# fp32 weight and Q/K loads by hardware DMA with casts on GpSimd, a mask added by a matmul, and global rows kept per parity, in a fused attention and feed-forward kernel

## The chip, the cores and the metric

The kernel runs on one core of a Trainium2 chip. The metric is device microseconds (us) of one execution. Before the change it takes 426.68 us in the median of 3 runs (426.24 to 429.5). Engines are named as the profile names them: PE (TensorE matmul), PEld (TensorE weight load), DVE (VectorE), ACT (ScalarE), POOL (GpSimd), SP (the queue that issues most DMAs).

## The reference, cut to what matters

```python
# attention: 8 batches, 8 heads, 576 positions, head dim 64
mask = np.abs(pos[:, None] - pos[None, :]) <= 32           # a band ...
mask = mask | is_global[:, None] | is_global[None, :]      # ... and 8 global positions
attn = softmax(where(mask, scale * q @ k.T, -1e9)); o = attn @ v
x = o.transpose(0, 2, 1, 3).reshape(4608, 512)
# feed-forward on 4608 tokens, 512 -> 1536 -> 512
ffn_out = (gelu(x @ w_gate) * (x @ w_val)) @ w_out
out = x + sigmoid(x @ w_res) * ffn_out
```

All inputs are fp32 in memory; the kernel computes in bf16.

## The kernel before: the parts that matter

The 4608 tokens are nine chunks of 512. For each chunk TensorE does twelve steps of the inner projections (`ffn_in`, matmuls into `g_ps` and `v_ps`), then sixteen pieces of the outer part (`r_ps`, three thirds of `f_ps` for each of four token tiles), and between those pieces the attention of the next chunk. Attention of a chunk needs scores `sc`, the scores of the global rows `sg` (keys of the global positions, `kgz`) and `ss` (queries of the global positions, `qgz`), and the values `nd`. A `gather` is an indirect DMA, issued by GpSimd, that fetches the rows at the global positions (`kgf`, `qgf`, `vgf`); `vgb` and `vgs` are the global rows of v in bf16 and spread over the heads. `hot` marks the global positions and `far` holds squared distances to them; both serve the masks.

```python
# loads that cast, issued by GpSimd
def load_gate_cols(n0, n1):
    for src, dst in ((moe_w_gate, wg_t), (moe_w_val, wv_t)):
        nc.gpsimd.dma_start(dst[:, :, n0:n1], src.rearrange(...)[:, :, n0:n1])
...
kgz = const.tile([128, B, NP, 128], BF16, ...)      # global rows of all 8 batches
qgz = const.tile([128, B, NP, 16], BF16, ...)
...
def shift_v(b):                                     # vo: ve moved by 64 partitions, by DMA
    nc.sync.dma_start(vo[b % 2][0:64, 0:4], ve[b % 2][64:128, 0:4])
    nc.sync.dma_start(vo[b % 2][64:128, 0:4], ve[b % 2][0:64, 1:5])
...
# scores: exp, then VectorE multiplies by the 0/1 mask
nc.scalar.activation(mine, sc, ACTF.Exp, bias=0.0, scale=SCALE)
nc.vector.tensor_tensor(mine, mine, view(maskw, ...), ALU.mult)
...
# spread_qk, once for batches 2 to 7 in chunk 1, by VectorE (k) and ScalarE (q)
(nc.scalar.copy if what == "q" else nc.vector.tensor_copy)(view(big, ...), view(tg, ...))
```

The softmax here doesn't subtract the row's maximum and nothing guards it: scores larger than these inputs give would overflow.

Of the kernel before, what the change touches and what calls it, by code (L numbers as in the profile page):

```python
# [23 lines left out]
def kernel(  # L24
# [46 lines left out]
    ve = pair_of([128, 5, H, VG], "ve")  # L71
    vo = pair_of([128, 4, H, VG], "vo")
# [5 lines left out]
    vgs = const.tile([128, B, H * VG], BF16, name="vgs", tag="vgs")  # L78
# [14 lines left out]
    def load_v(b):  # L93
        t = ve[b % 2]
        for c in range(5):
            p0, p1 = (32, 128) if c == 0 else (0, 96) if c == 4 else (0, 128)
            s0 = 128 * c - 32
            nc.gpsimd.dma_start(t[p0:p1, c, :, 0:D],  # L98
                                v[b].rearrange("h s d -> s h d")[s0 + p0:s0 + p1])

    def shift_v(b):
        nc.sync.dma_start(vo[b % 2][0:64, 0:4, :, :], ve[b % 2][64:128, 0:4, :, :])
        nc.sync.dma_start(vo[b % 2][64:128, 0:4, :, :], ve[b % 2][0:64, 1:5, :, :])

    def load_gate_cols(n0, n1):
        for src, dst in ((moe_w_gate, wg_t), (moe_w_val, wv_t)):
            nc.gpsimd.dma_start(dst[:, :, n0:n1], src.rearrange("(kt p) n -> p kt n", p=128)[:, :, n0:n1])


    RPP = 6  # L110
    QP = S // RPP
    STG = 2 * RPP * D
    raw = {"q": ht.rearrange("p a b -> p (a b)").bitcast(F32), "k": wo_t.rearrange("p a b -> p (a b)").bitcast(F32)}
# [3 lines left out]
    for p in range(NP):  # L117
        for src, what in ((q, "q"), (k, "k")):
            nc.sync.dma_start(raw[what][0:QP, STG * p:STG * p + STG].rearrange("c (h n) -> c h n", h=2),
                              src[0, 2 * p:2 * p + 2].rearrange("h (c r) d -> c h (r d)", r=RPP))  # L120

# [29 lines left out]
    kgz = const.tile([128, B, NP, 128], BF16, name="kgz", tag="kgz")  # L151
    qgz = const.tile([128, B, NP, 16], BF16, name="qgz", tag="qgz")

    def zero_qk(i):
        for u in range(2):
            zero_wide(qz[i], 64 - 64 * u, 64, u * S, [[2 * S, NP], [1, S]])
        zero_wide(kt[i], 0, 128, 0, [[S + 64, NP], [1, 32]])
        zero_wide(kt[i], 0, 128, 32 + S, [[S + 64, NP], [1, 32]])

    def zero_rest(i, eng):  # L160
        eng.memset(ve[i][:, :, :, D:VG], 1.0)
        eng.memset(ve[i][0:32, 0, :, :], 0.0)
        eng.memset(ve[i][96:128, 4, :, :], 0.0)
        eng.memset(gt[i][:, 0:64], 0.0)
        eng.memset(gt[i][:, 64 + S:128 + S], 0.0)
        eng.memset(ptg[i][:, :, 64 * (i % 2):64 * (i % 2) + 64], 0.0)

    def zero_globals(b0, b1):
        zero_wide(kgz, 0, 128, b0 * NP * 128, [[1, (b1 - b0) * NP * 128]])
        zero_wide(qgz, 0, 128, b0 * NP * 16, [[1, (b1 - b0) * NP * 16]])  # L170
# [5 lines left out]
    nc.scalar.copy(view(pt.bitcast(F32), 0, 128, 32, [[64, H * CH], [1, 32]]),  # L176
                   view(none, 0, 128, 0, [[0, H * CH], [0, 32]]))
# [3 lines left out]
    zero_qk(0)  # L181
    zero_globals(0, 2)
# [14 lines left out]
    zero_rest(0, nc.gpsimd)  # L197
    load_v(0)
    gather("v", 0)
    load_gate_cols(0, 512)  # L200


    gpc = const.tile([128, 1], F32, name="gpc", tag="gpc")
    nc.vector.tensor_copy(gpc, gpi)
    ngp = const.tile([128, 1], F32, name="ngp", tag="ngp")
    nc.vector.tensor_single_scalar(ngp, gpc, -1.0, ALU.mult)
    hot = const.tile([128, S], BF16, name="hot", tag="hot")
    nc.vector.tensor_scalar(hot, iota_f, gpc, None, ALU.is_equal)
    for n in range(1, B // 2):
        nc.vector.tensor_single_scalar(idx[:, n:n + 1], idx[:, 0:1], float(2 * H * S * n), ALU.add)  # L210
    far = const.tile([128, S], F32, name="far", tag="far")
# [5 lines left out]

    def masks():
        nc.vector.tensor_tensor(diag, blk[:, 0:8], blk[:, 8:16], ALU.add)
# [4 lines left out]
        for w0, w1 in ((0, NW), (NW, NWM)):  # L224
            n = w1 - w0
            nc.vector.tensor_tensor(maskw[:, w0:w1, :], nong[:, 0:64 * n].rearrange("p (w c) -> p w c", c=64),
                                    view(band, 0, 128, 0, [[0, n], [1, 64]]), ALU.mult)

    def hot_rows(i):
        r0 = 64 - 64 * (i % 2)  # L230
        nc.scalar.copy(gt[i][r0:r0 + 64, 64:64 + S], hot[r0:r0 + 64, :])
# [11 lines left out]
    def spread_qk(n0, n1):  # L243
        nn = n1 - n0
        for what, big, pstep in (("k", kgz, 144), ("q", qgz, 16)):
            tg = pss.tile([128, nn, 128], BF16, name="tg", tag="sc")
            for n in range(nn):
                nc.tensor.transpose(tg[:, n, :], twice[what][:, n0 + n, :, :].rearrange("p a d -> p (a d)"), ident)
            width = big.shape[2] * big.shape[3]
            for e in range(2):  # L250
                shift = 64 * e if what == "k" else 0
                for u in range(2):
                    (nc.scalar.copy if what == "q" else nc.vector.tensor_copy)(
                        view(big, 64 * u, 64, (2 * n0 + e) * width + shift + 8 * u,
                             [[2 * width, nn], [pstep, NP], [1, NG]]),
                        view(tg, 64 * u, 64, 64 * e + 8 * u, [[128, nn], [16, NP], [1, NG]]))
# [4 lines left out]
    def spread_vg(b, eng):  # L261
        r0 = 64 * (b % 2)
        eng.tensor_tensor(vgs[r0:r0 + 64, b, :].rearrange("p (h e) -> p h e", e=VG),
# [12 lines left out]
    def cast_pair(p, what):  # L276

        if p < 3:
            dst = (q_st if what == "q" else k_st).rearrange("c r n -> c (r n)")[0:QP, STG * p:STG * p + STG]
        else:  # L280
            o = 0 if what == "q" else STG
            dst = xtok[1].rearrange("c t n -> c (t n)")[0:QP, o:o + STG]
        src = raw[what][0:QP, STG * p:STG * p + STG].rearrange("c (u r d) -> c r u d", u=2, r=RPP)
        (nc.scalar.copy if what == "q" else nc.vector.tensor_copy)(dst.rearrange("c (r u d) -> c r u d", r=RPP, u=2), src)
        return dst

    def turn_pair(p, what, src):
        ps = bank([128, RPP, QP], f"t{what}0", BF16)
        for r in range(RPP):
            nc.tensor.transpose(ps[:, r, :], src[:, 128 * r:128 * r + 128], ident[0:QP, 0:QP])  # L290
        if what == "q":
            nc.scalar.copy(qt[0][:, p, :].rearrange("c (s r) -> c s r", r=RPP), ps.rearrange("c r s -> c s r"))
        else:
            nc.vector.tensor_copy(kt[0][:, p, 32:32 + S].rearrange("c (s r) -> c s r", r=RPP),
                                  ps.rearrange("c r s -> c s r"))
# [13 lines left out]
    def global_scores(b):  # L309
        sg = psn.tile([128, 2, 512], F32, name="sg", tag="nd")  # L310
        for hf in range(2):
            for p in range(NP):
                nc.tensor.matmul(sg[:, hf, 0:288], kgz[:, b, p, :], qt[b % 2][:, p, 288 * hf:288 * hf + 288],  # L313
                                 start=(p == 0), stop=(p == NP - 1))
        ss = pss.tile([128, 5, 64], F32, name="ss", tag="sc")
        for c in range(5):
            for p in range(NP):
                nc.tensor.matmul(ss[:, c, 16 * p:16 * p + 16], kt[b % 2][:, p, 128 * c:128 * c + 128],  # L318
                                 qgz[:, b, p, :], start=True, stop=True)
# [11 lines left out]
    def global_rows(b):  # L331
# [6 lines left out]
        nc.vector.tensor_tensor(vgs[rq:rq + 64, b, :].rearrange("p (a h e) -> p a h e", a=2, e=VG),  # L338
# [4 lines left out]
    def scores(c, quad, p):  # L343
        sc = bank([128, 4, 2, 64], "sc") if c == 0 else pss.tile([128, 4, 2, 64], F32, name="sc", tag="sc")
        for n in range(4):
            b, i = divmod(CH * c + 4 * quad + n, NW)
            nc.tensor.matmul(sc[:, n, :, :], kt[b % 2][:, p, 64 * i:64 * i + 128],  # L347
                             qz[b % 2][:, p, :, 64 * i:64 * i + 64], start=True, stop=True)
        mine = view(pt, 0, 128, (2 * p * CH + 4 * quad) * 128, [[128, 4], [CH * 128, 2], [1, 64]])
        nc.scalar.activation(mine, sc, ACTF.Exp, bias=0.0, scale=SCALE)  # L350
        i0 = (CH * c + 4 * quad) % NW
        nc.vector.tensor_tensor(mine, mine, view(maskw, 0, 128, 64 * i0, [[64, 4], [0, 2], [1, 64]]), ALU.mult)  # L352

    def values(c, t):
# [10 lines left out]
        for hf in range(2):  # L365
            for n, (b, c0) in enumerate(parts):
                nc.tensor.matmul(nds[hf][:, 0:HV], gt[b % 2][:, c0:c0 + 128], vgs[:, b, HV * hf:HV * hf + HV],  # L367
# [22 lines left out]
    def turn_x(c, t):  # L390
        mine = xt[c % 2][:, :, 128 * t:128 * t + 128]
        if c and t < 3:
# [53 lines left out]
    cast = {}  # L446
    for p in range(NP + 1):
        if p < NP:
            for what in "qk":
                cast[what] = cast_pair(p, what), cast.get(what, (None,))[0]  # L450
        if p == 0:
            masks()
        if p == 1:
            nc.scalar.activation(far, iota_f, ACTF.Square, bias=ngp, scale=1.0)
        if p:
            for what in "qk":
                turn_pair(p - 1, what, cast[what][1 if p < NP else 0])
            prep_qz(0, p - 1, p)
    hot_rows(0)
    double_qk(0, 1)  # L460
    spread_qk(0, 1)
    nc.vector.scalar_tensor_tensor(maskg, far, 1024.5, nong, ALU.is_gt, ALU.mult)
    shift_v(0)
    sg, ss = global_scores(0)
    global_exp(0, sg, ss)
    scores(0, 0, 0)
    spread_v(0, 1)
    spread_vg(0, nc.gpsimd)
    load_gate_cols(512, 1024)
    for p in range(1, NP):  # L470
        scores(0, 0, p)
    global_rows(0)
    load_qk(1)
    load_gate_cols(1024, 1536)
    zero_rest(1, nc.gpsimd)
    load_v(1)
    nc.gpsimd.dma_start(wr_t, moe_w_res.rearrange("(kt p) n -> p kt n", p=128))
    for h0 in range(0, NFF, 6):
# [96 lines left out]
```

## Time and profile before

| | before |
|---|---|
| span of the profiled execution | 425.2 us |
| TensorE busy, mean granted clock | 92%, 0.985 |
| feed-forward of chunk 0 starts | 34.28 |
| feed-forward of chunk 1 starts | 92.39, so 58.11 later |
| from there to the end | 332.8 |

The start of chunk 0's and chunk 1's feed-forward part is the first matmul into `g_ps` of that chunk. The three stages, start, chunk 0 and the rest, are limited by different things: the start by a chain through all engines, chunk 0 by loads, the rest by TensorE alone.

### The profile page before, as it was taken

What the parts mean: (1) busy time and instruction counts of PE and PEld (TensorE: products, weight loads), DVE (VectorE), ACT (ScalarE), POOL (GpSimd) and SP (SyncE); (2) the same over time, 40 slices, a digit from 0 to 9 for tenths busy, and PEclk for the clock granted to TensorE, in tenths of its full rate; (3) what the DMA queues carried; (4) which work ended last, traced back from release to release, by engine and by line L of the source; (5) the groups of instructions that cost most, each with busy time, mean ns of one, the idle gap of its engine ahead of it and who ended that gap; (6) DMA issues with size and microseconds to landing.
All of it is one profiled execution on the core that took longest, in us unless ns stands there. A gap on an engine that the chain in (4) does not pass through costs nothing.

```text
span 425.2 us, 7233 instructions
## 1 busy us (share of the span) xinstructions
PE 390.8 (92%) x2794; PEld 209.4 (49%) x2794; DVE 208.7 (49%) x390; ACT 169.8 (40%) x274; POOL 170.3 (40%) x200
## 2 busy tenths in 40 slices
PE   2578675999999999999999999999999999999994
PEld 1364232644565456545644564456445654564442
DVE  6776340535664356435644564456335633453321
ACT  5455241324543354335433542363336333524320
POOL 6678352952963461455144624452410220022012
PEclk9999995999999999999999999999999999999998
DMA  7999999999592995499339943991393130031001
GB/s 172 160 186 154 163 155 196 93 162 142 88 137 75 132 197 64 81 169 177 42 98 123 190 59 100 141 188 39 101 147 70 39 100 1 2 86 52 0 26 74
DMA packets 164643, 46.56 MB, mean 109 GB/s; under 512 B 152129, under 2 KB 158785, under 8 KB 164609
## 3 DMA queue, kind: packets, MB, share of 16 engines
q0 software_dynamic: 108784, 18.62, 60.9%
q1 hardware_dynamic: 55824, 27.48, 33.9%
q8 instruction: 22, 0.36, 0.4%
q14 instruction: 13, 0.10, 0.1%
HBM read 39.19 MB, written 9.44 MB: 114 GB/s over the span
## 4 chain that ended last, share of the span: by engine, by line
PE 72%; DMA 14%; issue 8%; DVE 2%; POOL 2%; SPq 1%; ACT 0%; POOLq 0%; DVEq 0%
PE f_ps L432 19%; PE g_ps L405 16%; PE v_ps L409 16%; PE r_ps L422 6%; DMA wv_t<-in_moe_w_val_dram 5%; DMA wo_t<-in_moe_w_out_dram 5%; PE nd L373 4%; PE sc L347 3%; DMA wo_t<-in_k_dram 2%; PE nd L367 2%; PE sg L313 2%; PE sn L335 2%; POOL ob L438 1%; DVE qz L306 1%; PE ss L318 1%
## 5 line engine op out<-in xcount | busy, mean ns | idle before, releaser
L413 DVE SCALAR_TENSOR_TENSOR ht<-gsb,v_ps 128x512 bf16<-128x512 bf16 x108 | 74.1, 688 | 98.8 <-PE v_ps L409 97.1
L438 POOL TENSOR_TENSOR ob<-prb,xtok 128x512 f32<-128x512 f32 x36 | 41.9, 1170 | 184.6 <-DVE prb L436 181.4
L412 ACT ACTIVATE gsb<-g_ps 128x512 bf16<-128x512 f32 x108 | 64.5, 597 | 128.1 <-PE g_ps L405 128.1
L405 PE MATMUL g_ps<-xt,wg_t 128*128 128x512 bf16 x432 | 110.9, 379 | 2.7 <-DMA wg_t<-in_moe_w_gate_dram 1.3
L409 PE MATMUL v_ps<-xt,wv_t 128*128 128x512 bf16 x432 | 110.9, 379 | 2.2 <-DMA wv_t<-in_moe_w_val_dram 2.1
L432 PE MATMUL f_ps<-wo_t,ht 128*128 128x512 bf16 x432 | 107.7, 384 | 5.2 <-DMA wo_t<-in_moe_w_out_dram 5.2
L409 PEld LDWEIGHTS <-wv_t 128*128 128x128 bf16 x432 | 42.2, 98 | 53.6 <-DMA wv_t<-in_moe_w_val_dram 2.5
L405 PEld LDWEIGHTS <-wg_t 128*128 128x128 bf16 x432 | 42.1, 98 | 53.8 <-issue 2.0
L432 PEld LDWEIGHTS <-ht 128*128 128x128 bf16 x432 | 38.8, 99 | 40.3 <-DMA wo_t<-in_moe_w_out_dram 5.3
L350 ACT ACTIVATE pt<-sc 128x512 bf16<-128x512 f32 x72 | 41.9, 597 | 37.3 <-PE sc L347 37.2
L352 DVE TENSOR_TENSOR pt<-pt,maskw 128x512 bf16<-128x512 bf16 x72 | 32.1, 448 | 36.7 <-ACT pt L350 35.6
L425 ACT ACTIVATE rsb<-r_ps 128x512 bf16<-128x512 f32 x36 | 21.4, 596 | 63.6 <-PE r_ps L422 55.8
L436 DVE SCALAR_TENSOR_TENSOR prb<-rsb,f_ps 128x512 f32<-128x512 bf16 x36 | 24.6, 685 | 29.4 <-PE f_ps L432 29.2
L90 POOL DMA_DIRECT2D q_st<-in_q_dram x35 | 30.0, 872 | 22.6 <-DMA qt<-q_st 22.6
L422 PE MATMUL r_ps<-wr_t,xt 128*128 128x512 bf16 x144 | 37.0, 379 | 1.9 <-DMA wr_t<-in_moe_w_res_dram 1.9
L98 POOL DMA_DIRECT2D ve<-in_v_dram x40 | 34.3, 869 | 1.0 <-DMA k_st<-in_k_dram 1.0
L90 POOL DMA_DIRECT2D k_st<-in_k_dram x35 | 30.7, 903 | 5.1 <-DMA kt<-k_st 2.9
L347 PEld LDWEIGHTS <-kt 128*128 128x128 bf16 x288 | 22.3, 102 | 12.7 <-issue 1.1
L347 PE MATMUL sc<-qz,kt 128*128 128x128 bf16 x288 | 28.5, 228 | 0.0
L387 DVE TENSOR_TENSOR xtok<-nd,rden 128x512 bf16<-128x512 f32 x34 | 23.5, 691 | 1.2
L373 PEld LDWEIGHTS <-pt 128*128 128x128 bf16 x576 | 22.3, 97 | 1.7 <-DMA vo<-ve 0.7
L373 PE MATMUL nd<-ve,pt 128*128 128x65 bf16 x320 | 22.4, 193 | 0.0
(98 smaller groups left out, 260.9 us busy)
## 6 DMA issues: line engine op xcount, KB each, us to landing
out_dram<-ob SPq DMA_DIRECT2D x36, 256.0 KB, 2.1
vo<-ve SPq DMA_DIRECT2D x16, 260.0 KB, 6.0
q_st<-in_q_dram POOLq DMA_DIRECT2D x28, 128.0 KB, 4.9
k_st<-in_k_dram POOLq DMA_DIRECT2D x28, 128.0 KB, 6.2
ve<-in_v_dram POOLq DMA_DIRECT2D x24, 128.0 KB, 7.3
ve<-in_v_dram POOLq DMA_DIRECT2D x16, 96.0 KB, 6.0
wg_t<-in_moe_w_gate_dram POOLq DMA_DIRECT2D x3, 512.0 KB, 6.2
wv_t<-in_moe_w_val_dram POOLq DMA_DIRECT2D x3, 512.0 KB
```

Of the source, the lines that this page charges most:

```text
L90: nc.gpsimd.dma_start(dst[0:n, r, :].rearrange("p (h d) -> p h d", d=D), src[b].rearrange("h s d -> s h d")[128 * r:128 * r + n])
L98: nc.gpsimd.dma_start(t[p0:p1, c, :, 0:D], v[b].rearrange("h s d -> s h d")[s0 + p0:s0 + p1])
L347: nc.tensor.matmul(sc[:, n, :, :], kt[b % 2][:, p, 64 * i:64 * i + 128], qz[b % 2][:, p, :, 64 * i:64 * i + 64], start=True, stop=True)
L350: nc.scalar.activation(mine, sc, ACTF.Exp, bias=0.0, scale=SCALE)
L373: nc.tensor.matmul(nds[h // 4][:, VG * (h % 4):VG * (h % 4) + VG], view(pt, 0, 128, c0, [[1, 128]]), vw, start=False, stop=(h % 4 == 3 and ...
L405: nc.tensor.matmul(g_ps, wg_t[:, kk, 128 * j:128 * j + 128], x[:, kk, :], start=(kk == 0), stop=(kk == NKT - 1))
L409: nc.tensor.matmul(v_ps, wv_t[:, kk, 128 * j:128 * j + 128], x[:, kk, :], start=(kk == 0), stop=(kk == NKT - 1))
L412: nc.scalar.activation(gsb, g_ps, ACTF.Gelu, bias=0.0, scale=1.0)
L413: nc.vector.scalar_tensor_tensor(ht[:, j, :], gsb, 0.5, v_ps, ALU.mult, ALU.mult)
L422: nc.tensor.matmul(r_ps, xt[c % 2][:, kk, 128 * t:128 * t + 128], wr_t[:, kk, :], start=(kk == 0), stop=(kk == NKT - 1))
L432: nc.tensor.matmul(held["f"], ht[:, j, 128 * t:128 * t + 128], wo_t[:, j, :], start=(j == 0), stop=(j == NFF - 1))
L438: nc.gpsimd.tensor_tensor(ob, prb, xtok[c % 2][:, t, :], ALU.add)
```

## The change

Its intent: let the hardware DMA queue load weights, Q/K of batches 0 and 1 and V of batch 0 as plain fp32, mostly into tiles that are not yet in use, and cast them in SBUF, mostly on GpSimd (Q/K of batch 0 were loaded so before, but cast by VectorE and ScalarE). The move of `vo` for batch 0 becomes two VectorE copies. In chunk 0 the mask becomes a bias that a matmul with the identity adds to the scores, in place of a product on VectorE. `kgz`, `qgz` and `vgs` are kept for two batches (per parity) rather than for eight, so they are filled for each batch. The scores of chunk 1 move into one block ahead of chunk 0's output pieces.

```diff
-    def load_gate_cols(n0, n1): ...
+    def load_piece(n):
+        nc.sync.dma_start(staged(n), pieces[n][0])      # 20 pieces of 512 KB, fp32
+    def cast_piece(n, copy):
+        copy(pieces[n][1], staged(n))
...
+        if c == 0:
+            nc.tensor.matmul(sc, ident, view(hide, ...), start=True, stop=False)
...
-    kgz = const.tile([128, B, NP, 128], ...)
+    kgz = pair_of([128, NP, 128], "kgz")
...
+    gather("v", 0)                      # now behind the casts of q and k
+    zero_v(0, nc.gpsimd)
...
+    for c in range(5):
+        cast_v(c, POOL)
     sg, ss = global_scores(0)
     global_exp(0, sg, ss)
-    shift_v(0)                          # (stood earlier)
+    for par in range(2):
+        DVE(vo[0][64 * par:64 * par + 64, 0:4], ve[0][64 - 64 * par:128 - 64 * par, par:4 + par])
     spread_v(0, 1)
-    spread_vg(0, nc.gpsimd)
+    spread_vg(0, nc.vector)
     global_rows(0)
+    for n in range(10):
+        cast_piece(n, POOL)
...
                 if j == 8:
                     shift_v(b)
                     if b + 1 < B:
                         load_qk(b + 1)
                     prep_qz(b, 0, NP)
+                if j == 9:
+                    spread_qk(b, compact, (b // 2) * 128, {"k": POOL, "q": POOL})
+                    spread_vg(b, nc.gpsimd)
```

## The prediction

> **What bounds the kernel now.** I read the slices of the page first, then the chain in order of time, then the instructions of TensorE and GpSimd in order of time. In the slices (one is 10.6 us) the engine row and the clock row matter:
>
> ```profile
> PE   2578675999999999999999999999999999999994
> PEclk9999995999999999999999999999999999999998
> DMA  7999999999592995499339943991393130031001
> ```
>
> After slice 8 TensorE is full. All loss is in the first 92 us. Stage by stage (columns: stretch, its length, busy us of PE, PEld, DVE, ACT, POOL with counts, clock, DMA share, GB/s):
>
> ```profile
> 4.00:6.00 2.00, 0.33 (x2) 0.11 (x1) 1.74 (x13) 0.11 (x1) 0.74 (x1) 1.00 1.01 279
> 8.00:10.00 2.00, 1.01 (x11) 0.58 (x8) 1.58 (x4) 1.75 (x3) 1.85 (x7) 1.00 1.09 253
> 60.00:64.00 4.00, 1.06 (x17) 0.60 (x14) 0.88 (x2) 1.68 (x3) 3.05 (x3) 1.00 1.31 201
> 135.00:177.00 42.00, 42.00 (x309) 22.75 (x307) 21.14 (x37) 17.55 (x28) 17.55 (x19) 1.00 1.13 117
> ```
>
> A steady chunk is 42.2 us of TensorE without a gap (chunk starts 135.28, 177.47, 219.45), so a new wait there is lost in full. The first two rows give the rate of plain fp32 loads, 250 to 280 GB/s; the third is a casting load, counted by its bf16 bytes, so it reads some 400 GB/s of fp32. In the early part of the chain two transfers are long (columns: start, us, what):
>
> ```profile
> 37.46 15.09 DMA wv_t<-in_moe_w_val_dram
> 52.84 20.69 DMA wo_t<-in_moe_w_out_dram
> 73.57 1.01 PE f_ps L432 x2
> ```
>
> TensorE pays for them here (start, busy, idle before it):
>
> ```profile
> 34.28 1.02 PE L405 MATMUL g_ps<-xt,wg_t 128*128 128x512 bf16 x4 [0.67 <-ACT xt L398]
> 52.60 1.04 PE L409 MATMUL v_ps<-xt,wv_t 128*128 128x512 bf16 x4 [2.06 <-DMA wv_t<-in_moe_w_val_dram]
> 70.25 1.89 PE L432 MATMUL f_ps<-wo_t,ht 128*128 128x512 bf16 x4 [5.00 <-DMA wo_t<-in_moe_w_out_dram]
> 92.39 1.02 PE L405 MATMUL g_ps<-xt,wg_t 128*128 128x512 bf16 x4 [0.77 <-DMA xt<-xtok]
> ```
>
> The feed-forward part starts at 34.28 and chunk 1 at 92.39, 58.1 us for what takes 42.2 later: some 16 us wait for weights and for batch 1. That is the most that better loading can win, plus what can be cut from the first 34 us.
>
> **What the Trainium skill says.** "DMA: Bandwidth & Descriptors", SWDGE vs HWDGE, says that a DMA that casts must be issued by GpSimd; the trace agrees, each weight load has a GpSimd issue of 0.8 us and each q/k/v load one of 0.87. The same page, Issuing engines are not separate DMA queues, says all issuers share 16 engines; so the change moves bytes but adds no bandwidth. "GPSIMD Engine Reference", section 3.1, puts simple bodies at about 1.03 cycles an element and two-input ones at 2.6; here the two-input 128x512 add took 1170 ns, or about 2.3 ns an element, which fits 2.6 at its 1.2 GHz, but no GpSimd copy is in this trace. "SBUF — State Buffer", Who interferes with whom, says GpSimd and some VectorE forms lock each other out; the trace before does not isolate it.
>
> **The change part by part.**
>
> (1) Start. Casts of batch 0 go from 96-row pairs shared by VectorE and ScalarE (0.56 and 0.83 us) to nine 128x512-wide copies on GpSimd and one on VectorE. Estimate of a GpSimd copy from the skill's 1.03 cycles: 0.86 ns an element plus about 0.1 us (the 32x520 memset took 0.52 us), so 0.6 us for 512 and 1.0 for 1024. GpSimd, free at about 7 us after the two gathers (1.43 and 0.97), does nine in 5.5 us, ends near 14 with the last landing, then has the memsets, hot rows, far, its square and the gather (about 6.5 us), and six casts of v (3.5 us): 24. The bias by matmul removes eight mask multiplies of 0.42 us from VectorE and adds eight 512-wide matmuls of 0.22 us to TensorE, both before that point, so beside it. After 24: two copies for vo, two vgs of 0.7, then four value tiles limited by VectorE at about 1.1 each, the last transpose and copy, 1. The feed-forward part starts near 32.5 instead of 34.3: gain 1.8.
>
> (2) Weights of the inner part. Twelve pieces of 524 KB, at 260 GB/s 2.0 us each, against 1.73 us of TensorE per piece (24 groups of four matmuls, 0.864 us, in 20.7 us). Batch 0's q and k are 2.36 MB (9 us), v 1.18 MB (5 to 6), so piece 0 lands at about 20 and piece 11 near 44, cast by 46; TensorE wants it at 50. The waits of 1.25 and 2.06 us, and the later ones for wr and wo, go away only if that rate holds.
>
> (3) Batch 1. Its q and k are turned on TensorE between the last inner steps. After piece 11 GpSimd has memsets 1.4, load of v 4.3, k casts 3: ready at 51 to 54, wanted from 50. I book 2 us for these waits and the transposes. The scores of chunk 1 are no longer spread between output thirds, but come in one run: one table load of 1.28, eight exps of 0.6, 0.44 and 0.63 for the globals, one tanh of 0.6, and the chain through the last pair before them: 11 us in which TensorE has about 5 of work. If the inner part ends at 55, scores and globals end at 66; then 15 groups of 0.864, values 2.9 and transposes 0.9 make 16.8: chunk 1 at 83.
>
> (4) The bytes. Up to the last piece of wo, 2.36+1.18+6.29+2.36+4.19 = 16.4 MB, at 260 GB/s 63 us, plus 3 at the start and some 6 for v of batch 1 and for 256-byte rows: 72, cast by 73. It is wanted at about 69. So chunk 1 starts at 83 + 4 = 87: gain 5 to 6 us of the 16.
>
> (5) Global rows per parity. Now each batch's kgz and qgz are filled by four small copies on GpSimd, in program order behind load_qk of the next batch. The order of instructions shows it: ten q/k loads, then kgz, and the first matmul of sg waits for that count of GpSimd. In the trace before, ends of the last k load against sg:
>
> ```profile
> 156.24 0.70 POOL L90 DMA_DIRECT2D k_st<-in_k_dram  x1 [0.35 <-issue]
> 156.00 1.14 PE L313 MATMUL sg<-qt,kgz 128*128 128x288 bf16 x8
> 238.62 3.32 POOL L90 DMA_DIRECT2D k_st<-in_k_dram  x4 [0.69 <-DMA kt<-k_st]
> 240.17 1.14 PE L313 MATMUL sg<-qt,kgz 128*128 128x288 bf16 x8
> ```
>
> Loads end 0.94, 1.05, 1.77 and 0.18 us after sg wants to start, in the four chunks from 135 on; before, nothing on TensorE cared. With two copies of about 0.3 us behind them, TensorE waits 1.5, 1.6, 2.4 and 0.8: 6.3 us. In chunk 1 six gathers at 1.35 (8.1), v 4.3 and ten loads 8.7 follow the last add, which ends 1.3 after the chunk's start: 22.4, kgz at 23, wanted at 21.1: 1.9 more. Chunks 6 to 8 load no further q and k and wait for nothing. Sum 8.2 us lost.
>
> Sum: 426.7 - 5.4 - 0.8 (the wait for xt at 92.39) + 8.2 = about 428.5; I write 428.
>
> **The rivals.** First, loading pays and the steady wait does not come: if GpSimd's issues finish a little earlier, or sg is not held, the time is 420 or, at 300 GB/s and more in the loads, 416. For it speaks that larger plain transfers may run better than the measured 96-row ones; against it that ten issues of 0.87 us are in the trace and the order of GpSimd is fixed. Second, GpSimd becomes the bound of the first chunk: if a 1024-wide cast takes 1.75 us instead of 1.0, 20 of them cost 15 us more, v is cast at 27.5, batch 1's k at 58, and chunk 1 starts near 90: 432; with locks against VectorE's copies 435. Third, the transfers bound it: at 220 GB/s the last piece lands at 83 and chunk 1 starts at 97, after the 13 us of work behind it: 438. The measured 250 speaks against that, the slower 256-byte rows of v for it.
>
> **Range and chances.** The gain at the start is 0 to 10 us, the steady loss 4 to 11; the two are nearly independent, so most of the mass lies within 2% (418.1 to 435.2), with a little more above than below: 417 to 438 for 8 in 10, 0.13 faster, 0.70 same, 0.17 slower.
>
> **What would show it.** Right: chunk 1 starts at 83 to 92; TensorE idle before sg, released by kgz on GpSimd, 1 to 2 us in each of chunks 1 to 5 and none in 6 and later; steady chunks of 43 to 44 us before that and 42 after. A GpSimd cast of 128x1024 near 1.0 us; f_ps of chunk 0 still waiting for the last pieces of wo; waits on k_st casts in the last inner steps. Wrong: chunk 1 before 80, or no wait at sg (then it is faster by over 2%), or a chunk 1 after 95 with idle TensorE released by GpSimd casts or plain weight loads (then slower).

## The result

The changed kernel takes **448.44 us** (447.17 to 450.14, 4 runs) against 426.84 us (426.24 to 429.5, 4 runs) for the kernel before: slower, ratio 1.05 with a 95% interval of 1.045 to 1.055. A ratio here is the mean time of one kernel's fast runs over the mean of the other's fast runs of the same rounds, so it is not quite the ratio of the medians. The profiled execution: span 445.4, mean clock 0.966.

The slices of the page (one is now 11.1 us; same three rows as in the prediction):

```profile
PE   2831897899979999999899999998999999999994
PEclk9965999999969999999999999999999999999998
DMA  8999997914991699369927993999298140021001
```

TensorE has a hole in the third and fourth slices (22 to 45 us) that was not there, the clock falls there too and once more in the twelfth, and after the eighth slice TensorE is no longer solidly at 9. By stages:

| | before | after | difference |
|---|---|---|---|
| start of chunk 0's feed-forward | 34.28 | 50.09 | +15.8 |
| from there to chunk 1's | 58.11 | 50.63 | -7.5 |
| from there to the end | 332.8 | 344.7 | +11.9 |
| span | 425.2 | 445.4 | +20.2 |

Chunk 0 gained what the change was for. The start and the steady part lost more.

**The start.** The chain of work that ended last, in order of time (start, us, what):

```profile
25.96 1.74 POOL ve L256 x3
27.71 11.90 DVE vo L558
39.65 1.42 DVE vo L558
41.10 0.25 DVE vgb L321
41.37 0.69 DVE vgs L325
42.09 0.71 DVE vgs L401
42.85 0.59 PE nd L435 x2
```

The first of the two `vo` copies took 11.90 us, the second, of the same size, 1.42. GpSimd meanwhile, instructions in order of time (start, busy, what, idle before it):

```profile
24.61 3.62 POOL L256 CAST ve<-vraw 32x512 bf16<-32x512 f32 x6 [3.21 <-DMA vgf<-in_v_dram,idx]
28.19 1.03 POOL L136 CAST wg_t<-qz 128x1024 bf16<-128x1024 f32 x1
...
38.03 1.03 POOL L136 CAST wg_t<-xt 128x1024 bf16<-128x1024 f32 x1
39.31 1.21 POOL L136 CAST wv_t<-xtok 128x1024 bf16<-128x1024 f32 x1 [0.25 <-DMA xtok<-in_moe_w_val_dram]
```

Eleven casts of weights ran without a gap, and the VectorE copy ended at 39.61, just after GpSimd paused for 0.25 us at 39.06 to wait for a transfer. On GpSimd's line there is also an idle time of 3.21 us ahead of the casts of v, put down to the gather `vgf`.

**Chunk 0 and the steady part.** TensorE, in order of time:

```profile
42.85 0.59 PE L435 MATMUL nd<-vgs,gt 128*128 128x260 bf16 x2 [13.97 <-DVE vgs L401]
50.09 1.02 PE L473 MATMUL g_ps<-xt,wg_t 128*128 128x512 bf16 x4 [0.68 <-ACT xt L466]
100.72 1.03 PE L473 MATMUL g_ps<-xt,wg_t 128*128 128x512 bf16 x4
125.60 2.10 PE L376 MATMUL sg<-qt,kgz 128*128 128x288 bf16 x8 [3.61 <-POOL kgz L317]
215.32 1.15 PE L376 MATMUL sg<-qt,kgz 128*128 128x288 bf16 x8 [1.67 <-POOL kgz L317]
344.05 1.14 PE L376 MATMUL sg<-qt,kgz 128*128 128x288 bf16 x8
```

The first line is TensorE's side of the long copy: 13.97 us of idle time. In chunk 0 it no longer waits for weights at all. From chunk 1 on, `sg` waits for `kgz` in five chunks; the view of waits sums them (engine, line, released by: total, times, longest):

```profile
PE sg L376 <- POOL kgz L317: 8.3, 5, 3.6
```

and the last line of the fence above it, chunk 6's `sg`, has none. What `kgz` stood behind on GpSimd in chunk 1:

```profile
124.37 0.69 POOL L92 DMA_DIRECT2D k_st<-in_k_dram  x1 [0.29 <-issue]
125.05 0.48 POOL L317 COPY kgz<-kgc 64x32 bf16<-64x32 bf16 x2
```

The copies themselves are small; they are late because GpSimd issues the ten loads of the next batch first. The matmuls after the longest wait ran slowly (2.10 us for what takes 1.14 elsewhere). The windows show why (stretch, length, busy us of PE, PEld, DVE, ACT, POOL, then granted clock, DMA share, GB/s):

```profile
20.00:27.00 7.00, 3.54 (x44) 2.48 (x42) 2.12 (x4) 2.80 (x6) 3.57 (x7) 0.93 1.09 346
117.00:125.00 8.00, 4.99 (x28) 2.20 (x26) 5.38 (x11) 3.07 (x4) 6.36 (x8) 1.00 2.04 169
124.94:131.77 6.83, 6.17 (x43) 3.64 (x44) 1.13 (x3) 2.53 (x5) 2.00 (x6) 0.50 1.48 122
131.77:140.00 8.23, 8.23 (x85) 5.49 (x84) 4.50 (x10) 3.75 (x7) 1.16 (x1) 1.00 0.09 34
```

For 6.83 us the clock was half; TensorE was busy for 6.17 of them, so about 3.1 us of work were lost besides the wait (an estimate; the expectation of e2_vector_spread below says 3.4 and 11.7, half of all 6.83 us, though 0.66 of them were still the wait). 8.3 and 3.1 make 11.4 of the 11.9 us of the steady loss. The Trainium skill, "TensorE: Matmul & The Clock Gate", Part 1, puts the clock at half after an idle window of about 3.4 us and back after a busy window of that length, and says that these windows run freely. This trace agrees: the 3.61 us wait was followed by half clock, the waits of 0.8 to 1.7 us were not, and the half clock lasted 6.83 us, about two such windows, of which the first still held 0.66 us of the wait. The first row is the rate of the plain weight loads, 346 GB/s.

So there are two theories to test. **A: the start lost its time to the long copy**, because VectorE was kept out by GpSimd's run of casts. The Trainium skill, "SBUF — State Buffer", Who interferes with whom, says that GpSimd and VectorE share one port pair as an exclusive lock: VectorE's copies and casts in their two-port modes, and its instructions with two SBUF inputs, block or are blocked "for the whole instruction". **B: the steady part lost its time to the order on GpSimd**, `kgz` behind ten loads. Rivals: that the copy is slow by itself (64x2080 elements that cross partitions); that TensorE would wait anyway for casts of weights; that a VectorE fill of `kgz` delays something else; and that some third loss is hidden beneath these two.

### The profile page after: what moved, and what is told of

The parts are those of the page before. It is cut to its first block, busy times and chain, and to the rows that moved or that the text cites. A ratio compares the mean times of both kernels' runs of the same rounds, so it can differ in the third digit from the quotient of the medians.

```text
span 445.4 us, 7416 instructions
## 1 busy us (share of the span) xinstructions
PE 399.4 (90%) x2846; PEld 214.6 (48%) x2846; DVE 222.1 (50%) x400; ACT 169.7 (38%) x275; POOL 188.7 (42%) x239
## 4 chain that ended last, share of the span: by engine, by line
PE 49%; issue 22%; DMA 11%; POOL 10%; DVE 5%; ACT 2%; SPq 1%; POOLq 0%; ACTq 0%
PE f_ps L500 13%; PE g_ps L473 10%; PE v_ps L477 9%; DMA kt<-k_st 5%; PE r_ps L490 4%; POOL ob L506 3%; PE nd L441 3%; DVE vo L558 3%; PE sc L413 3%; POOL k_st L92 2%; DMA qt<-q_st 2%; PE sg L376 2%; DMA ve<-in_v_dram 2%; PE nd L435 2%; PE sn L398 2%
## 5 line engine op out<-in xcount | busy, mean ns | idle before, releaser
L500 PE MATMUL f_ps<-wo_t,ht 128*128 128x512 bf16 x432 | 105.9, 381 | 0.0
L420 DVE TENSOR_TENSOR pt<-pt,maskw 128x512 bf16<-128x512 bf16 x64 | 27.2, 425 | 28.1 <-ACT pt L416 26.5
L92 POOL DMA_DIRECT2D q_st<-in_q_dram x30 | 25.7, 877 | 34.2 <-DMA qt<-q_st 24.1
L100 POOL DMA_DIRECT2D ve<-in_v_dram x35 | 29.9, 871 | 0.0
L435 PE MATMUL nd<-vgs,gt 128*128 128x260 bf16 x80 | 15.5, 285 | 14.0 <-DVE vgs L401 14.0
L92 POOL DMA_DIRECT2D k_st<-in_k_dram x30 | 26.7, 900 | 3.0 <-DMA kt<-k_st 2.3
L441 PEld LDWEIGHTS <-pt 128*128 128x128 bf16 x576 | 23.3, 99 | 1.3
```

Source lines behind the costliest of these rows:

```text
L92: nc.gpsimd.dma_start(dst[0:n, r, :].rearrange("p (h d) -> p h d", d=D), src[b].rearrange("h s d -> s h d")[128 * r:128 * r + n])
L100: nc.gpsimd.dma_start(t[p0:p1, c, :, 0:D], v[b].rearrange("h s d -> s h d")[s0 + p0:s0 + p1])
L441: nc.tensor.matmul(nds[h // 4][:, VG * (h % 4):VG * (h % 4) + VG], view(pt, 0, 128, c0, [[1, 128]]), vw, start=False, stop=(h % 4 == 3 and ...
L500: nc.tensor.matmul(held["f"], ht[:, j, 128 * t:128 * t + 128], wo_t[:, j, :], start=(j == 0), stop=(j == NFF - 1))
```

## The experiments

All outputs are right. The kernel before took 427.17 us in the rounds of the first four runs (7 runs), 427.37 in those of the next four (7) and 426.79 in the last two (11). Where an interval below lies wholly under 1, the difference is clear of noise. There is no e9 on record.

### e1_pause: GpSimd waits before the weight casts

```diff
-    spread_vg(0, nc.vector)
+    spread_vg(0, nc.gpsimd)
```

`vgs` needs `vgb`, which VectorE makes after the `vo` copies. Put on GpSimd ahead of the weight casts, it makes GpSimd stand still while the copies run. No copy is changed.

> The product vgs of batch 0 goes from VectorE to GpSimd, ahead of the twelve weight casts, so GpSimd must stop until VectorE has done the two vo copies and the vgb cast. Port theory (VectorE's copy of 11.90 us only waited for GpSimd's run of casts to leave the port they share): the two vo copies take about 0.7 us each (at most 1.4), the feed-forward part starts near 39 instead of 50.1, time near 437. Rival (the copy of 64x2080 between partition halves is slow by itself, or v is what is late): the copies still take over 10 us, the feed-forward part still starts near 50, and the time stays 448 or rises by the 1.2 us of the product on GpSimd.

Measured: 437.26 us (436.62 to 440.2), ratio 1.0267 (1.0211 to 1.0324). The copies and the stop on GpSimd:

```profile
28.17 1.80 DVE L558 COPY vo<-ve 64x2080 bf16<-64x2080 bf16 x2 [3.16 <-POOL ve L256]
30.28 1.05 POOL L325 TENSOR_TENSOR vgs<-vgb,diag 64x520 bf16<-64x520 bf16 x1 [1.59 <-DVE vgb L321]
```

Both copies together now took 1.80 us instead of 13.36. The feed-forward part started at 38.72 instead of 50.09, chunk 1 at 89.64, so chunk 0 still takes 50.9. The copy is not slow by itself, and TensorE did not wait for weight casts that were pushed back by 3 us. Half the loss, 11.2 us, is this.

### e2_vector_spread: kgz and qgz filled by VectorE and ScalarE

```diff
-                    spread_qk(b, compact, (b // 2) * 128, {"k": POOL, "q": POOL})
+                    spread_qk(b, compact, (b // 2) * 128, {"k": DVE, "q": ACT})
```

> The four small copies into kgz and qgz of batches 2 to 7 go from GpSimd to VectorE (k) and ScalarE (q); nothing else changes. Theory of the steady wait: TensorE no longer waits before sg (8.3 us in five chunks), and the half clock from 124.9 to 131.8, which the 3.6 us wait of chunk 1 brought (3.4 us of work lost), goes too: 448.4 less 11.7 is 436.7, and chunk 1 to the end takes 332.8 as before the change. Rival (sg waits for the transposed q and k anyway, the copies only come last by the profile): the wait stays at 1 to 3 us a chunk and the time above 443.

Measured: 437.48 us (436.94 to 439.69), ratio 1.0267 (1.0215 to 1.0318). No `sg` waits, and chunk 1's runs at full clock:

```profile
122.21 1.15 PE L376 MATMUL sg<-qt,kgz 128*128 128x288 bf16 x8
```

Chunk 1 started at 101.10 and the rest took 334.1, against 344.7. Of that gain of 10.6 us 8.3 are the waits; the other 2.3 are about the 3.1 of the clock less one new wait of 0.9 us, for a transposed `kt`.

### e3_scalar_vo: the copies on ScalarE

```diff
-        DVE(vo[0][...], ve[0][...])
+        ACT(vo[0][...], ve[0][...])
```

> Only the two vo copies go from VectorE to ScalarE; vgb's cast and the product vgs stay on VectorE beside the casts of GpSimd. Port theory: ScalarE's copies take about 1.9 us each (a 128x2048 copy took 1.90 there) and are done by 32; but the wait moves to the next VectorE instruction that needs the shared port, the cast of vgb or the two-input product vgs, one of which then takes up to 11 us. If those get in before the casts of GpSimd, the feed-forward part starts near 40 and the time is 438; if not, 446 to 449. Rival (the copy is slow by itself on VectorE): ScalarE does it in 4 us, no other VectorE instruction grows, time 438.

Measured: 436.26 us in one run. The copies took 3.87 us on ScalarE, and the start was 39.78. But it does not separate the causes as I had meant, because the next VectorE instructions, which I had expected to be held up, had slipped in ahead of the weight casts (which start at 29.38):

```profile
27.30 0.60 DVE L321 CAST vgb<-vgf 128x64 bf16<-128x64 f32 x1
27.93 1.02 DVE L325 TENSOR_TENSOR vgs<-vgb,diag 64x520 bf16<-64x520 bf16 x1
```

They ran beside the casts of v and each got its turn there, at a price: the six casts of v took 4.31 us instead of 3.62. So a run of GpSimd casts does not always keep VectorE out until it ends.

### e4_pause_later: the same stop after six of the casts

```diff
-    spread_vg(0, nc.vector)
...
         cast_piece(n, POOL)
+        if n == 5:
+            spread_vg(0, nc.gpsimd)
```

If the run of casts is what holds VectorE, half the run should hold it half as long.

> As e1_pause, but GpSimd's product vgs stands behind six of the twelve casts. Port theory: the first vo copy ends when those six casts are done, at 28.2 + 6 x 0.98 = 34.1, so it takes about 6.5 us instead of 11.9, and the feed-forward part starts near 45: time about 443. Rival (the copy is slow by itself): still 11 to 12 us.

Measured: 444.15 us in one run, start 44.82. The sixth cast and VectorE:

```profile
33.01 1.03 POOL L136 CAST wv_t<-kt 128x1024 bf16<-128x1024 f32 x1
27.60 6.75 DVE L392 TENSOR_TENSOR gt<-gt,maskg 64x576 bf16<-64x576 bf16 x1 [3.61 <-ACT gt L390]
34.38 1.42 DVE L558 COPY vo<-ve 64x2080 bf16<-64x2080 bf16 x2
```

The dose came out: VectorE was free again at 34.35, 0.3 us after the sixth cast ended at 34.04. Which instruction was held was a surprise: not the copy but the product before it, which has two SBUF inputs and takes 0.45 us elsewhere. After the casts the two copies took 1.42 together. The start gained 5.3 us and the whole 4.3: chunk 0 took 51.94, 1.3 longer, with one wait of 1.16 us of TensorE that was not traced. With e1_pause this shows the run of casts as the cause of the long copy; that the shared port is the way it acts is the skill's account quoted above, which no run here isolates.

### e5_both: e1 and e2 together

The edit is that of e1_pause and that of e2_vector_spread.

> e1_pause and e2_vector_spread in one. If the two losses are separate and are all that the change lost, the gains add: 448.4 - 11.2 - 11.0 = 426.3, the same as the kernel before, with the feed-forward part at 39, chunk 1 at 90 and 333 us after it. Rival (one wait hides the other, or a third loss stands behind them): 430 or more.

Measured: 425.82 us (425.19 to 426.99), ratio 0.9978 (0.9933 to 1.0024), the same as before. Alone the two edits gained 11.2 and 11.0 us, together 22.6; the change had lost 21.6. So the two losses add, and neither hides the other. The start is 39.25 (before: 34.28), chunk 0 takes 50.88 (58.11), the rest 334.2 (332.8): minus 7.2, plus 5.0 and plus 1.4. The repaired change only moves time from one stage to another: a loss of 5.0 us is left in the start, and what chunk 0 gained covers it.

### e6_both_early: v's global rows gathered earlier

```diff
+    gather("v", 0)
     zero_gt(0, nc.gpsimd)
     hot_rows(0)
     nc.gpsimd.tensor_scalar(far, iota_f, gpc, None, ALU.subtract)
     nc.gpsimd.tensor_tensor(far, far, far, ALU.mult)
-    gather("v", 0)
```

Of the 5.0 us that remain in the start, 3.6 stand in e5_both ahead of v's casts, put down to this gather.

> As e5_both, with GpSimd's gather of v's global rows moved ahead of the memsets, hot rows and far, so that its landing no longer holds the casts of v (3.2 us idle on GpSimd before them in the changed kernel). Theory: v is cast 3 us earlier, and so is all behind it: 423. Rival (v's own rows land no earlier than 24): no gain, 426.

Measured: 424.45 us (424.23 to 424.78), ratio 0.9942 (0.9901 to 0.9983): 1.4 us better, less than expected. The wait had only moved, to a copy that reads nothing of the gather:

```profile
19.59 0.66 POOL L289 COPY gt<-hot 64x576 bf16<-64x576 bf16 x1 [3.07 <-DMA vgf<-in_v_dram,idx]
```

My reason, that it is the casts of v that need the gather, was wrong. Why this copy waits I did not find out; it isn't every instruction behind a gather, since in e10_start below the casts of q and k follow v's gather without a wait.

### e7_both_early_mult: the first chunk masked by products again

```diff
-        if c == 0:
+        if False:
             nc.tensor.matmul(sc, ident, view(hide, ...), start=True, stop=False)
...
-        if c == 0:
-            return
         nc.vector.tensor_tensor(mine, mine, view(maskw, ...), ALU.mult)
```

> As e6_both_early, but the first chunk is masked as before the change: no matmul that adds the bias, eight VectorE products of 0.42 us with maskw instead. Theory (the scores lie beside the wait for v, so the bias matmul gains nothing): same time as e6 within 1 us, though the products have two SBUF inputs and may wait for GpSimd's casts, or hold them, up to 2 us. Rival (the bias matmul takes 3.4 us of VectorE off the path): 426 to 427.

Measured: 426.14 us (425.27 to 426.5), ratio 0.9977 (0.9934 to 1.0019), 1.7 us more than e6_both_early, with no overlap of the runs. The start moved from 38.31 to 40.09. The mask by matmul is worth 1.7 us in this version, half of what the eight products of 0.42 us add up to, so the theory missed and the rival's time came. How it does so is not shown: in the two traces 0.7 us of it stands on GpSimd ahead of v's casts, where the wait put down to the gather is 4.26 us instead of 3.07.

### e8_woven: chunk 1's attention spread between chunk 0's output pieces

The change had put the scores of chunk 1 in one block. This run spreads them over the sixteen output pieces, as in all later chunks.

```diff
-            for n in range(2):
-                scores(1, 0, n)
-            global_exp(1, *held)
-            ...
+            jobs[0].append(global_exp_1)
+            jobs[4].append(lambda: global_rows(1))
+            for n in range(8):
+                jobs[n].append(lambda n=n: scores(1, n // 4, n % 4))
+            ...
```

> As e6_both_early, with chunk 1's scores, globals and values woven between the output thirds of chunk 0 as in all later chunks, instead of in one run ahead of them. Theory: the 3.4 us in which TensorE waits for ScalarE between the scores go, if the last pieces of wo are cast by then (about 64): 419.5. Rival (wo comes too late for an earlier start): TensorE waits for the casts of wo instead, 422 to 424.

Measured: **421.1 us** (420.99 to 421.42), ratio 0.9866 (0.9825 to 0.9907). Chunk 0 takes 47.25 us (39.07 to 86.32) instead of 50.9. This version beats both kernels, by 1.3% against the one before, though its start is still 4.8 us later than before the change. In e5_both, TensorE had waited three times for some 0.6 to 0.7 us for ScalarE's exps in the block; those waits are gone, which is 2.0 of the 3.6 us; where the rest was I did not trace.

### e10_start and e11_start_far: two attempts on the start

```diff
     gather("k", 0)
     gather("q", 0)
+    gather("v", 0)
...
-    gather("v", 0)
```

> The woven version with v's gather issued directly behind the first gather of q. Theory: the wait of 3.07 us that stood ahead of GpSimd's first copy out of the hot rows is the landing of the gathers, so issuing v's gather earlier makes it land before that copy; the values' casts and everything behind start about 2.5 us earlier, feed-forward at about 36.5 instead of 39.1, and the time is about 418.8 us (woven: 421.1). Rival: the bytes of the plain loads set when the gather lands, so moving its issue moves its landing little: 421. Second rival: the start gets earlier, but the casts of wo in chunk 0 then arrive too late and TensorE waits there for what was gained: 420 to 421 with a wait at the output matmul.

e11_start_far keeps that and computes `far` on ScalarE:

```diff
+    nc.scalar.activation(far, iota_f, ACTF.Square, bias=ngp, scale=1.0)
...
-    nc.gpsimd.tensor_scalar(far, iota_f, gpc, None, ALU.subtract)
-    nc.gpsimd.tensor_tensor(far, far, far, ALU.mult)
```

> As the run before it in this call, with the far mask computed by ScalarE's Square as in the kernel before, in place of the two GpSimd operations of 1.73 and 1.15 us. Theory: those 2.9 us stand on GpSimd ahead of the casts of v, so the start gets another 2 to 2.9 us shorter: about 416.3 us. Rival: v's landing or the plain loads bind by then, and the time stays at the run before's (about 418.8); the profile would show it as a wait for a DMA ahead of v's first cast, or ahead of chunk 0's weights.

Measured: 421.84 us (420.8 to 422.95), ratio 0.9883 (0.9841 to 0.9925), and 420.74 us (418.92 to 421.91), ratio 0.987 (0.9838 to 0.9902). Neither is told apart from e8_woven. The step on GpSimd came out: in e10_start the wait ahead of the hot rows is gone and v's casts start at 20.25 instead of 24.80. Yet TensorE's feed-forward part started at 39.52. None of the named rivals explains that; by the trace it looks like theory A again, in another place, but no run was made to test it. GpSimd's casts of q and k now ran without the pause for a transfer that they had in e8_woven, and a two-input product and copies of VectorE took longer beside them:

```profile
9.04 2.65 DVE L276 TENSOR_TENSOR maskw<-nong,band 128x576 bf16<-128x576 bf16 x1
13.32 2.51 DVE L370 COPY qz<-qt 64x576 bf16<-64x576 bf16 x2
11.34 0.83 POOL L344 CAST q_st<-ht 128x512 bf16<-128x512 f32 x1
13.85 0.61 POOL L344 CAST q_st<-ht 128x512 bf16<-128x512 f32 x1
```

The product took 0.46 us in e8_woven and the two copies 1.02. The product came through beside the cast at 11.34, the fifth of the run, which took 0.2 us longer than its like; the first `qz` copy, by the chain, not before 15.11, after the last cast had ended at 14.46. From 7.8 us on the chain of e10_start runs through VectorE, not GpSimd. In the profiled execution of e11_start_far the same product took 0.46 us, and feed-forward started at 35.35; that was its fastest run, 418.92 us. Its spread of 3 us, against 0.4 in e8_woven, fits a start that depends on who gets the port first in each run, but I have profiles of one run of each only, so this is not shown.

## Why the prediction was wrong

It said 428.0 us, within 2%; the result was 448.44, outside its range of 417 to 438.

- **Step (1), the start, failed.** Up to the landing of q and k it was right: GpSimd's casts of q and k ended at 14.2 (predicted near 14), a cast took 0.61 and 1.03 us (0.6 and 1.0). Then came "After 24: two copies for vo, two vgs of 0.7", which took the copies at their price on an idle port. The first measured 11.90 us; e1_pause, which changes no copy and makes GpSimd's casts wait, takes 11.2 us off the time. The rival "with locks against VectorE's copies 435" had the mechanism and gave it 3 us, where a run of eleven casts held one copy for 11.9; its own premise, a cast of 1.75 us, did not come (1.03). The other term that was missing is the gather: "24" was 28.2, of which 3.2 are the wait ahead of v's casts. Some 2 us more lie behind the copies: 9.0 us from there to the feed-forward part, where the step has about 7; the granted clock was 0.50 from 38 to 44 us, and what that cost was not tested. The prediction's own sign of being wrong, chunk 1 after 95, came (100.72), but the idle TensorE was released by VectorE, not by casts or loads.
- **Steps (2) and (3), weights and batch 1, held.** Chunk 0 took 50.63 us; step (3) has 50.5 (83 minus 32.5). The waits in its last inner steps, 0.50 and 0.67 us, were for ScalarE's copies of the turned q, not for k's casts, which the prediction's signs name.
- **Step (4), bytes, was off in size.** It added 4 us for a rate of 260 GB/s. The plain loads ran at 346 GB/s, and TensorE waited for no piece of `wo`.
- **Step (5), the wait for kgz, was right in place and lacked one term; that its sum fits is in part luck.** It has 8.2 us in chunks 1 to 5 (1.9, 1.5, 1.6, 2.4 and 0.8) and none from chunk 6; the trace has 8.3 (3.6, 0.8, 1.7, 0.8 and 1.5), and none. In chunk 1 the ten loads took 10.5 us, 114.5 to 125.1, where the step has 8.7, with a wait of 0.90 for a transfer among them. It did not ask what so long a wait does to the clock: about 3.1 us more. e2_vector_spread removes both, for 11.0 us.
- **"The bias by matmul" was called beside the path** with no gain of its own; e7_both_early_mult gives it 1.7 us.
- **"the two are nearly independent"** was right and is shown by e5_both; but the start's range of a gain of 0 to 10 us had no room for a loss, which is why the whole range was too narrow and "slower" got only 0.17.

Sum of the misses in the trace: the start 50.1 instead of 32.5, plus 17.6; chunk 0 50.6 instead of 54.5 (87 minus 32.5), minus 3.9; the steady part 11.9 instead of 8.2, plus 3.7. Together 17.4. The prediction's own sum has a slip: 426.7 - 5.4 - 0.8 + 8.2 is 428.7 (it writes 428.5), and it takes the 0.8 twice, since the start of chunk 1 at 92.39, from which it reckons the 5.4, already lies behind that wait. Without it the sum is 429.5, and 429.5 and 17.4 make 446.9. The trace grew by 20.2 us (425.2 to 445.4), and 426.7 and 20.2 make 446.9 too; the median grew by 21.6.

## What to carry to other kernels

Work that is given to an idle GpSimd has to be priced on VectorE too: look for VectorE copies, casts and two-input products that run at the same time as a long unbroken run of GpSimd instructions that read SBUF, and put a point between them where GpSimd waits; here one instruction moved to GpSimd did it, for 11.2 us. A small copy that TensorE needs must not stand behind a batch of DMA issues on the same engine, and a wait that is long enough to bring the clock down costs its length and then some (here 3.6 us and about 3.1 more). When a repaired change only moves time from one stage to another, look at each stage for what the change took away: here spreading chunk 1's scores again brought 3.4 us.

## What the Trainium skill lacked or had wrong

- "SBUF — State Buffer", Who interferes with whom: it names the right instructions, and VectorE was held, but it speaks of blocking "for the whole instruction". Here a VectorE instruction was held through many GpSimd instructions in a row: a copy 11.90 us, through the end of a cast of v and eleven casts of 1.03 us, a product 6.75 us through six. When VectorE gets in between is not stated, and the runs do not settle it: in e3_scalar_vo a product took its turn beside the casts of v (1.02 us), in e10_start another beside the fifth cast.
- "GPSIMD Engine Reference", section 3.1: it has no measured line for a cast or copy. Here a fp32 to bf16 cast took 0.61 us for 128x512 and 1.03 us for 128x1024, at a spacing of 0.56 and 0.98 us. A subtraction with an operand per partition took 1.73 us for 128x576 fp32, 3.0 ns an element, slower than the two-input product of the same size (1.15 us), and no figure there suggests it.
- No page has it: in e6_both_early a GpSimd copy waited 3.07 us for the landing of an indirect DMA whose data it does not read. It may be the program's wait and not the chip's.
